# Second layer of a mixture of experts: rows gathered two units ahead, and one shared part for full and small units

## The chip, the cores and the metric

The kernel runs on one core of a Trainium2 chip. The metric is the device time of one execution in microseconds; the time of a kernel is the median of several runs. The engines are named as in the profile: PE is TensorE's matmul, PEld its weight load, DVE VectorE, ACT ScalarE, POOL GpSimd, SP SyncE.

## What is computed

The reference is attention with pooled queries, then two dense layers with a piecewise activation, then a second mixture of experts. Only the last step is touched by the change:

```python
N, D = x.shape                      # 2304 tokens, 512 columns
expert_idx = np.argmax(logits, axis=1)          # one of 8 experts for each token
gate_w = probs[np.arange(N), expert_idx]
for e in range(E):
    mask = expert_idx == e
    h = np.maximum(x[mask] @ w1[e], 0.0)        # w1[e]: 512 x 1024
    out[mask] = gate_w[mask, None] * (h @ w2[e])  # w2[e]: 1024 x 512
```

All is fp32. The kernel splits each fp32 operand into a high part, rounded to the format that PE multiplies fast, and a low part, the rest; a product is three matmuls (high by high, high by low, low by high).

## The kernel before, in words

The first stages write the rows of x to a table in HBM and scatter, for each token, a record (row number, output row, gate) into a second table that is sorted by expert. `units()` cuts this table into units of 256 rows of one expert; how many units there are (9 to 17) and which expert each has is known only at run time. The last unit of an expert can have 128 rows or fewer; it is then a small unit. A bit mask `half`, held in registers, says which units are small.

`Moe2.run` is written out for 17 units in a row; from unit 9 on each stands in a conditional on the number of units. What one unit does:

- `gather(u)` (L1202) has SP load 256 records (L1210), and POOL gather the 256 rows of x in two indirect DMAs of 128 rows (L1220) into a ring of four buffers `d_xg`, followed by a drain of POOL (L1206).
- `nxt(u)` (L1313) calls `gather(u)`, then reads the expert and a flag on SP and loads the four raw pieces of w1 (`load("1")`, L1182); the DMA is conditional, since the expert may be the one that is already there. `load("2")` does the same for w2.
- `split` (L1184) turns one of the eight pieces of a raw weight matrix into its high part (a cast on ACT, L1187) and its low part (a subtraction on DVE, L1188). There is one set of high and low parts: w1 of the next unit is split while the second product runs, w2 of the unit itself while its first product runs.
- `x_t` (L1235) transposes the next unit's rows on PE (L1227) and evicts them as a high part on ACT (L1231) and a low part on DVE (L1232).
- `hidden(f, x)` (L1241) makes an eighth of the hidden layer of a full unit in 12 matmuls of 256 columns (L1248), with a relu on ACT (L1250) and the low part on DVE (L1251).
- `half(x)` (L1253) makes the whole hidden layer of a small unit in 24 matmuls of 512 columns (L1262), with the rows on the partitions; `turn(i)` (L1270) transposes half of it (L1274).
- `outer(t, f)` (L1279) adds an eighth of the second product of tile t (128 rows) in three matmuls of 512 columns (L1284). `store` (L1288) scales the result on ACT (L1291) and has POOL scatter it to the output (L1292). A store waits for the landing of the one before.

The order is the program's order on each engine. In a unit u from 1 on, `nxt(u + 1)` comes first; then stands a conditional with two arms (L1335). The full arm has 8 `hidden`, 8 `outer(0, f)` with `x_t` behind f = 0 and a w1 split behind each f, a store, 8 `outer(1, f)`, a store. The small arm has `half`, 8 `outer(0, f)` with the second turn behind f = 1, `x_t` behind f = 5 and the same splits, and one store. Each engine evaluates the conditional by itself and jumps over the arm that is not taken. Unit 0 is always full and is written out apart; while it runs, the units are still being counted.

Of the kernel before, what the change touches and what calls it, by code (L numbers as in the profile page):

```python
# [11 lines left out]
U32 = mybir.dt.uint32  # L12
# [17 lines left out]
UMAX = UMIN + E  # L30
# [44 lines left out]
class Attention:  # L75
# [11 lines left out]
    def open(self, ctx):  # L87
        tc, nc = self.tc, self.nc

        def pool(name, bufs, **kw):  # L90
            return ctx.enter_context(tc.tile_pool(name=name, bufs=bufs, **kw))

        self.prep = tc.alloc_tile_pool(name="a_prep", bufs=1, side="right")
        self.vp = pool("a_v", 1)
        self.ktp = pool("a_kt", 2)
        self.sp = pool("a_s", 3)
        self.sm = pool("a_sm", 3)
        one = pool("a_one", 1)
        self.ps_s = pool("a_ps_s", 1, space=PSUM)
        self.ps_a = pool("a_ps_a", 1, space=PSUM)  # L100
        self.ps_b = pool("a_ps_b", 1, space=PSUM)
        self.ps_v = pool("a_ps_v", 2, space=PSUM)
        self.pth = one.tile([128, 9, RING], F32R, name="pth")
        self.ptl = one.tile([128, 9, RING], F32R, name="ptl")
        self.vh = one.tile([128, 18, 128], F32R, name="vh")
        self.avs = one.tile([128, 2 * NQ], F32, name="avs")

        self.qts = [one.tile([128, 2, QW], F32R, name=f"qt{i}") for i in range(2)]

        self.bd = [one.tile([128, 2, 128], F32R, name=f"bd{i}") for i in range(2)]  # L110
        self.kk = one.tile([128, 2, S], F32R, name="kk")
        self.r = one.tile([128, 32], F32, name="r")
        self.nc.vector.memset(self.r, 1.0)
# [1012 lines left out]
class Moe2:  # L1126
# [63 lines left out]
    def open(self, ctx):  # L1190
        def pool(name, **kw):
            return ctx.enter_context(self.tc.tile_pool(name=name, bufs=1, reuse_waits="tile", **kw))

        p, ps = pool("d_sb"), pool("d_ps", space=PSUM)
        self.ph = Ring(ps, 3, [128, 512], F32, "d_ph")
        self.pt = Ring(ps, 2, [128, 4, 128], F32, "d_pt")
        self.po = Ring(ps, 3, [128, 512], F32, "d_po")
        self.rec = Ring(p, 3, [128, 2, 4], U32, "d_rec")
        self.xg = Ring(p, 4, [128, DM], F32, "d_xg")
        self.ob = Ring(p, 4, [128, DM], F32, "d_ob")  # L1200

# [75 lines left out]
        nc.vector.tensor_sub(out=l, in0=p, in1=h.bitcast(F32))  # L1277

    def outer(self, t, f):  # L1279
        if f == 0:  # L1280
            self.o = self.po()
        s = slice(t * 128, t * 128 + 128)
        for q, (a, b) in enumerate(((0, "2h"), (0, "2l"), (1, "2h"))):
            self.nc.tensor.matmul(self.o, lhsT=(self.hh, self.hl)[a][f // 4][:, f % 4, s],  # L1284
                                  rhs=self.w[b, f // 2][:, f % 2],
                                  start=f == 0 and q == 0, stop=f == 7 and q == 2)
# [9 lines left out]
    def run(self, items):  # L1296

        nc, tc, rt = self.nc, self.tc, self.rt
        evs = []
        rec, x = self.rec0, self.xt0  # L1300

        def routing():
            while evs:
                evs.pop(0)()
            while items:
                f = items.popleft()
                if f is None:
                    return
                e = f()
                if e:  # L1310
                    evs.append(e)

        def nxt(u):  # L1313
            r = self.gather(u)
            e = nc.sync.value_load(rt.u[0:1, u, 1:2], min_val=0, max_val=E - 1)
            c = nc.sync.value_load(rt.u[0:1, u, 2:3], min_val=0, max_val=1)
            self.load("1", e, c)
            return r, e, c

        first = []  # L1320

        def step():
            if next(steps, None):
                first.extend(nxt(1))

        with ExitStack() as ifs:  # L1326
            for u in range(UMAX):
                if u >= UMIN:
                    ifs.enter_context(tc.If(total > u))
                more = u + 1 < UMAX  # L1330
                if more and u:
                    (rec1, xs1), e, c = nxt(u + 1)
                if u:
                    x1 = (self.xh(), self.xl()) if more else None
                    with tc.If((half & (1 << u)) == 0) as full:  # L1335
                        for f in range(8):
                            self.hidden(f, x)
                            self.split("2", f)
                        if more:
                            self.load("2", e, c)  # L1340
                        for f in range(8):
                            self.outer(0, f)
                            if more:
                                if f == 0:
                                    self.x_t(xs1, x1)
                                self.split("1", f)
                        self.store(rec, 0)
                        for f in range(8):
                            self.outer(1, f)
                        self.store(rec, 1)  # L1350
                    with full.Else():
                        self.half(x)
                        if more:
                            self.load("2", e, c)
                        for f in range(8):
                            self.outer(0, f)
                            if f == 1:
                                self.turn(1)
                            if more:
                                if f == 5:  # L1360
                                    self.x_t(xs1, x1)
                                self.split("1", f)
                        self.store(rec, 0)
                    x = x1
                else:
                    for f in range(2, 8):
                        self.hidden(f, x)
                        routing()
                        if f == 4:
                            steps = rt.units()  # L1370
                        for _ in range(min(3, f - 3)):
                            if not first:
                                step()
                        for i in {4: (2, 3), 5: (4, 5), 6: (6, 7)}.get(f, ()):
                            self.split("2", i)
                    for f in range(8):
                        self.outer(0, f)
                        step()
                    self.store(rec, 0)
                    self.load("2", *first[1:])  # L1380
                    for f in range(6):
                        self.outer(1, f)
                        step()
                    while not next(steps, 1):
                        pass
                    (rec1, xs1), e, c = first
                    for f in (0, 2, 4, 6):
                        self.split("1", f)
                    x = self.xh(), self.xl()
                    self.x_t(xs1, x, lambda: self.outer(1, 6))  # L1390
                    self.outer(1, 7)
                    total = nc.values_load(rt.u[0:1, 0, 2:3], min_val=UMIN, max_val=UMAX)
                    half = nc.values_load(rt.half[0:1, 0:1], min_val=0, max_val=(1 << (UMAX + 1)) - 1)
                    for f in (1, 3, 5, 7):
                        self.split("1", f)
                    self.store(rec, 1)
                if more:
                    rec = rec1

# [133 lines left out]
```

## Time and profile before

| | us |
|---|---|
| median of three runs | 1179.3 |
| lowest and highest run | 1173.73, 1179.88 |
| the profiled execution, its own time | 1178.18 |
| its span, first to last instruction | 1176.4 |

The profile is of one execution. Its times count from the start of the span. The granted clock of TensorE was 0.995 of full speed over the span. The second layer, from unit 1's start at about 938 us to the end, is a fifth of the span.

### The profile page before, as it was taken

The page shows a single profiled execution, that of the slowest core. Times are in us where ns is not written, and L with a number is a line of the kernel's source. Part 1 is how long each engine was busy: PE and PEld are TensorE (multiplying, and loading weights), DVE is VectorE, ACT ScalarE, POOL GpSimd, SP SyncE. Part 2 cuts the span into 40 slices and gives each one's busy share as a digit, 9 for nine tenths or more (in the row PEclk, how much of TensorE's full clock was granted, in tenths as well). Part 3 has the DMA queues.
Part 4 walks back from the last instruction along what each step waited for, and adds up shares of the span by engine and source line. Part 5 has one row for each costly group of instructions (what it writes and reads, how often), then busy time and mean ns, then how long its engine had stood idle before and what let it go on. Part 6 is the DMA issues. An engine that isn't in the chain of part 4 may idle for free. (4 is left out here: it accounts for less than half of the span.)

```text
span 1176.4 us, 21181 instructions
## 1 busy us (share of the span) xinstructions
PE 1135.4 (97%) x7315; PEld 1056.2 (90%) x7315; DVE 883.1 (75%) x1593; ACT 753.2 (64%) x1477; POOL 580.7 (49%) x499
## 2 busy tenths in 40 slices
PE   7999999999999999799999999999999999999997
PEld 6999999999999999799789999998889899887886
DVE  6898898899999998698866664764355776676765
ACT  5888888887878787555554445544435566566764
POOL 6998988887888885267762121112010221121212
PEclk9999999999999999899999999999999999999999
DMA  7777777786868758354532222120222121286443
GB/s 181 175 186 180 175 168 175 172 212 134 207 163 204 168 139 177 101 170 152 161 113 67 59 69 73 41 68 20 90 82 100 45 64 38 80 271 208 158 140 122
DMA packets 87877, 156.14 MB, mean 133 GB/s; under 512 B 26535, under 2 KB 44967, under 8 KB 87744
## 3 DMA queue, kind: packets, MB, share of 16 engines
q1 hardware_dynamic: 83040, 142.34, 45.4%
q0 software_dynamic: 4336, 11.58, 3.0%
q8 instruction: 67, 1.10, 0.4%
q10 hardware_dynamic: 368, 0.59, 0.2%
q14 instruction: 66, 0.54, 0.2%
HBM read 145.84 MB, written 20.08 MB: 141 GB/s over the span
## 5 line engine op out<-in xcount | busy, mean ns | idle before, releaser
L236 DVE TENSOR_SCALAR_CACHE_REDUCE e<-sc 128x1152 f32<-128x1152 f32 x144 | 194.7, 1352 | 24.3 <-PE sc L232 23.0
L243 ACT ACTIVATE e<-e,nm 128x1152 f32<-128x1152 f32 x144 | 183.6, 1275 | 9.0 <-DVE e L236 8.9
L232 PE MATMUL sc<-kT,qt 128*128 128x384 f32 x780 | 160.1, 340 | 11.7 <-DVE e L236 9.6
L270 ACT CAST pth<-pa 128x768 fp32r<-128x768 f32 (+2 forms) x160 | 116.3, 737 | 78.6 <-PE pa L261 78.4
L272 DVE TENSOR_TENSOR ptl<-pa,pth 128x768 fp32r<-128x768 f32 (+2 forms) x160 | 138.8, 876 | 17.7 <-ACT pth L270 5.5
L1188 DVE TENSOR_TENSOR e<-e,e 128x512 fp32r<-128x512 f32 x200 | 129.5, 688 | 28.3 <-ACT e L1187 12.3
L232 PEld LDWEIGHTS sc<-kT,qt 128*128 128x128 f32 x780 | 132.8, 189 | 14.5 <-DVE e L236 11.7
L596 DVE SCALAR_TENSOR_TENSOR u<-h,u 128x320 f32<-128x320 f32 (+1 forms) x112 | 55.7, 497 | 107.8 <-ACT u L595 107.4
L592 ACT ACTIVATE u<-h,half 128x320 f32<-128x320 f32 (+1 forms) x112 | 59.7, 533 | 109.5 <-PE h L577 109.3
L1284 PE MATMUL d_po<-e,e 128*128 128x512 f32 x504 | 121.0, 393 | 0.6 <-DVE e L1188 0.6
L261 PE MATMUL pa<-idf,e 128*128 128x128 f32 x864 | 117.6, 272 | 3.0 <-DVE ptl L272 3.0
L1187 ACT CAST e<-e 128x512 fp32r<-128x512 f32 x200 | 113.7, 619 | 0.6 <-issue 0.3
L609 PE MATMUL y<-wh,gh 128*128 128x512 f32 x288 | 113.9, 395 | 0.0
L609 PE MATMUL y<-wh,gl 128*128 128x512 f32 x288 | 113.7, 395 | 0.0
L609 PE MATMUL y<-wl,gh 128*128 128x512 f32 x288 | 113.6, 394 | 0.0
L261 PEld LDWEIGHTS pa<-idf,e 128*128 128x128 f32 x864 | 102.9, 140 | 8.3 <-issue 2.2
L1284 PEld LDWEIGHTS d_po<-e,e 128*128 128x128 f32 x504 | 92.6, 188 | 19.2 <-DVE e L1188 1.0
L1292 POOL DMA_INDIRECT out<-d_ob,d_rec x19 | 22.5, 1186 | 176.0 <-ACT d_ob L1291 119.3
L598 ACT CAST gh<-u 128x320 fp32r<-128x320 f32 (+1 forms) x112 | 52.3, 467 | 79.9 <-DVE u L596 79.9
L286 PE MATMUL av<-pth,vh 128*128 128x288 f32 x576 | 103.1, 306 | 0.0
L286 PE MATMUL av<-ptl,vh 128*128 128x288 f32 x576 | 102.2, 304 | 0.0
L577 PE MATMUL h<-xth,wh 128*128 128x320 f32 (+1 forms) x448 | 87.8, 318 | 8.3 <-DVE u L596 6.8
(258 smaller groups left out, 2533.8 us busy)
## 6 DMA issues: line engine op xcount, KB each, us to landing
e<-moe_w SPq DMA_DIRECT2D x104, 512.0 KB
kr<-k SPq DMA_DIRECT2D x63, 288.0 KB
qr<-q SPq DMA_DIRECT2D x62, 288.0 KB
kk<-kT SPq DMA_DIRECT2D x60, 288.0 KB
vr<-v SPq DMA_DIRECT2D x16, 576.0 KB
av_b<-avs SPq DMA_DIRECT2D x64, 128.0 KB
wi<-moe_w_in SPq DMA_DIRECT2D x16, 512.0 KB
wo<-moe_w_out SPq DMA_DIRECT2D x16, 512.0 KB
```

The costliest lines, as they stand in the source:

```text
L232: nc.tensor.matmul(s[:, j, 0:384], lhsT=a, rhs=b[:, 384 * j:384 * j + 384], start=i == 0, stop=i == len(mm) - 1)
L236: nc.vector.tensor_scalar(out=e.rearrange("p (a b) -> p a b", a=3), in0=s[:, :, 0:384], scalar1=-0.5 / D ** 0.5, scalar2=None, op0=ALU.mul ...
L243: self.nc.scalar.activation(e, e, AF.Exp, bias=d["nm"][:, t:t + 1], scale=-1.0, accum_out=d["sum"][:, t:t + 1])
L261: nc.tensor.transpose(p[:, c // 3, (c % 3) * 128:(c % 3) * 128 + 128], e[:, i * 128:(i + 1) * 128], idf)
L270: nc.scalar.copy(hi, p)
L272: nc.vector.tensor_sub(out=lo, in0=p, in1=hi.bitcast(F32))
L286: nc.tensor.matmul(box["t"][:, 0:GQ], lhsT=self.vh[:, h * 9 + i % 9], rhs=p[:, i % 9, c0:c0 + GQ], start=i == 0, stop=i == 17)
L577: nc.tensor.matmul(ps[:, :n], lhsT=a[:, k], rhs=b[:, k, h0:h0 + n], start=i == 0, stop=i == 11)
L609: self.nc.tensor.matmul(y, lhsT=a, rhs=b, start=j == 0 and q == 0, stop=j == NF - 1 and q == 2)
L1187: self.nc.scalar.copy(hi, r)
L1188: self.nc.vector.tensor_sub(out=lo, in0=r, in1=hi.bitcast(F32))
L1284: self.nc.tensor.matmul(self.o, lhsT=(self.hh, self.hl)[a][f // 4][:, f % 4, s], rhs=self.w[b, f // 2][:, f % 2], start=f == 0 and q == 0, ...
```

## The change

The rows of unit u + 2 are gathered in unit u, behind `nxt(u + 1)`, which no longer gathers; unit 0 ends with the gather of unit 2. The ring of records has four entries. The conditional's arms keep the first product, the load of w2 and the first two eighths of the second product of tile 0 (in the small arm with the second turn). The other six eighths, `x_t` (ahead of f = 4), the w1 splits (from f = 2 on) and the first store are written once, behind the arms. The second tile of a full unit stands in a second conditional. The PSUM bank of a second product is now taken by `run`, not by `outer`.

```diff
-        self.rec = Ring(p, 3, [128, 2, 4], U32, "d_rec")
+        self.rec = Ring(p, 4, [128, 2, 4], U32, "d_rec")
...
     def outer(self, t, f):
-        if f == 0:
-            self.o = self.po()
...
+        gathered = {}
+
         def nxt(u):
-            r = self.gather(u)
             e = nc.sync.value_load(rt.u[0:1, u, 1:2], min_val=0, max_val=E - 1)
             c = nc.sync.value_load(rt.u[0:1, u, 2:3], min_val=0, max_val=1)
             self.load("1", e, c)
-            return r, e, c
+            return e, c
...
             if next(steps, None):
+                gathered[1] = self.gather(1)
                 first.extend(nxt(1))
...
-                if more and u:
-                    (rec1, xs1), e, c = nxt(u + 1)
                 if u:
+                    if more:
+                        e, c = nxt(u + 1)
+                    if u + 2 < UMAX:
+                        gathered[u + 2] = self.gather(u + 2)
+                    rec1, xs1 = gathered.get(u + 1, (None, None))
                     x1 = (self.xh(), self.xl()) if more else None
+                    self.o = self.po()
                     with tc.If((half & (1 << u)) == 0) as full:
                         for f in range(8):
                             self.hidden(f, x)
                             self.split("2", f)
                         if more:
                             self.load("2", e, c)
-                        for f in range(8):
+                        for f in range(2):
                             self.outer(0, f)
-                            if more:
-                                if f == 0:
-                                    self.x_t(xs1, x1)
-                                self.split("1", f)
-                        self.store(rec, 0)
-                        for f in range(8):
-                            self.outer(1, f)
-                        self.store(rec, 1)
                     with full.Else():
                         self.half(x)
                         if more:
                             self.load("2", e, c)
+                        for f in range(2):
+                            self.outer(0, f)
+                        self.turn(1)
+                    for f in range(2, 8):
+                        if more:
+                            if f == 4:
+                                self.x_t(xs1, x1)
+                            for i in (0, 1) if f == 2 else (f - 1,):
+                                self.split("1", i)
+                        self.outer(0, f)
+                    if more:
+                        self.split("1", 7)
+                    self.store(rec, 0)
+                    with tc.If((half & (1 << u)) == 0):
+                        self.o = self.po()
                         for f in range(8):
-                            self.outer(0, f)
-                            if f == 1:
-                                self.turn(1)
-                            if more:
-                                if f == 5:
-                                    self.x_t(xs1, x1)
-                                self.split("1", f)
-                        self.store(rec, 0)
+                            self.outer(1, f)
+                        self.store(rec, 1)
                     x = x1
...
                     self.store(rec, 1)
+                    gathered[2] = self.gather(2)
```

## Rows read from the trace of the kernel before

**Rows 1.** The page's first part: busy us, share of span, instructions.

```profile
PE 1135.4 (97%) x7315; PEld 1056.2 (90%) x7315; DVE 883.1 (75%) x1593; ACT 753.2 (64%) x1477; POOL 580.7 (49%) x499
```

**Rows 2.** Stretches of units 3, 5, 7, 9, 11: us; busy PE, PEld, DVE, ACT, POOL; clock; DMA share.

```profile
984.13:1007.20 23.07, 23.07 (x153) 21.14 (x152) 15.04 (x26) 13.74 (x28) 4.34 (x4) 1.00 0.15 48
...
1030.45:1045.90 15.45, 12.94 (x66) 10.81 (x66) 10.44 (x17) 11.58 (x22) 3.39 (x3) 1.00 0.74 241
...
1069.10:1084.90 15.80, 13.24 (x66) 10.69 (x66) 10.72 (x18) 11.60 (x22) 3.22 (x3) 1.00 0.70 227
...
1107.80:1122.20 14.40, 13.30 (x66) 10.59 (x65) 10.76 (x18) 11.65 (x22) 3.06 (x3) 1.00 0.76 264
...
1145.10:1176.40 31.30, 23.68 (x153) 20.86 (x151) 15.13 (x26) 14.54 (x29) 5.90 (x5) 0.98 0.40 138
```

**Rows 3.** PE's waits from unit 1 on: us in total, times, longest.

```profile
PE d_ph L1262 <- ACT e L1187: 4.0, 2, 2.5
PE d_pt L1227 <- DMA d_xg<-y_rows,d_rec: 3.5, 4, 1.2
```

**Rows 4.** Timeline of PE: start, us, what, xcount, [idle before <- releaser].

```profile
1032.96 1.17 PE L1262 MATMUL d_ph<-e,d_xh 128*128 128x512 f32 x4 [2.51 <-ACT e L1187]
...
1039.00 1.54 PE L1284 MATMUL d_po<-e,e 128*128 128x512 f32 x6
...
1045.82 0.94 PE L1248 MATMUL d_ph<-d_xh,e 128*128 128x256 f32 x4
...
1070.61 1.17 PE L1262 MATMUL d_ph<-e,d_xh 128*128 128x512 f32 x4 [1.49 <-ACT e L1187]
...
1082.95 0.66 PE L1227 MATMUL d_pt<-idf,d_xg 128*128 128x128 f32 x4 [1.07 <-DMA d_xg<-y_rows,d_rec]
...
1107.81 1.08 PE L1262 MATMUL d_ph<-e,d_xh 128*128 128x512 f32 x4
...
1113.77 1.52 PE L1284 MATMUL d_po<-e,e 128*128 128x512 f32 x6
...
1119.45 1.44 PE L1227 MATMUL d_pt<-idf,d_xg 128*128 128x128 f32 x8 [0.97 <-DMA d_xg<-y_rows,d_rec]
...
1159.79 10.48 PE L1284 MATMUL d_po<-e,e 128*128 128x512 f32 x45
```

**Rows 5.** PE's branches at L1335, four windows: xcount, ns min/median/max, first and last start.

```profile
L1335 PEldq COMPARE_BRANCH  x2: 174/3200/6227, 1026.2 to 1026.6; - x2
...
L1335 PEldq COMPARE_BRANCH  x2: 312/2692/5072, 1064.9 to 1065.4; - x2
...
L1335 PEldq COMPARE_BRANCH  x2: 174/250/325, 1103.8 to 1104.2; - x2
...
L1335 PEldq COMPARE_BRANCH  x6: 66/128/312, 957.0 to 1003.6; - x6
```

**Rows 6.** The page's third part: packets, MB, share of 16 engines.

```profile
q8 instruction: 67, 1.10, 0.4%
```

**Rows 7.** Timeline of POOL in unit 7, and the landing of all gathers.

```profile
1073.82 1.00 POOL L1292 DMA_INDIRECT out<-d_ob,d_rec  x1 [7.73 <-DMA out<-d_ob,d_rec]
...
1076.67 0.97 POOL L1220 DMA_INDIRECT d_xg<-y_rows,d_rec  x1 [0.30 <-PE d_ph L1262]
...
DMA to landing us min/median/max: 3.2/3.9/6.5
```

**Rows 8.** Timelines of ACT and DVE in unit 9, behind the second turn.

```profile
1116.25 2.18 ACT L1187 CAST e<-e 128x512 fp32r<-128x512 f32 x4
...
1116.38 0.69 DVE L1277 TENSOR_TENSOR e<-d_pt,e 128x512 fp32r<-128x512 f32 x1
1116.99 2.49 DVE L1188 TENSOR_TENSOR e<-e,e 128x512 fp32r<-128x512 f32 x4
```

**Rows 9.** Timeline of POOL, the last two stores.

```profile
1165.88 1.20 POOL L1292 DMA_INDIRECT out<-d_ob,d_rec  x1 [11.01 <-ACT d_ob L1291]
1171.27 1.00 POOL L1292 DMA_INDIRECT out<-d_ob,d_rec  x1 [4.19 <-ACT d_ob L1291]
```

More of the change, by code (lines that the diff above doesn't have):

```diff
@@ L1375, in run @@
                             self.split("2", i)
+                    self.o = self.po()
                     for f in range(8):
@@ L1379, in run @@
                     self.store(rec, 0)
-                    self.load("2", *first[1:])
+                    self.load("2", *first)
+                    self.o = self.po()
                     for f in range(6):
@@ L1385, in run @@
                         pass
-                    (rec1, xs1), e, c = first
                     for f in (0, 2, 4, 6):
                         self.split("1", f)
+                    rec1, xs1 = gathered[1]
                     x = self.xh(), self.xl()
```

## The prediction

> **What bounds the kernel now.** The page comes first: PE is busy for 97% of the span [rows 1], so time can be won only where PE waits or where the program ends after it. The change touches the second layer alone. The table of its stretches, cut at the units' borders, shows which units run: unit 0, then 1 to 4 full, 5 small, 6 full, 7 small, 8 full, 9 small, 10 and 11 full. A full unit has no idle PE (23.07 us of 23.07); the small ones idle 2.5, 2.6 and 1.1 us, and the last stretch 7.6 us, most of it the program's end [rows 2]. The list of PE's waits from unit 1 on has two rows only: two waits before the first product of a small unit, 4.0 us, and four waits of the transposes for gathered rows, 3.5 us [rows 3]. The timeline places them: 2.51 us at the start of unit 5 and 1.49 at that of 7, but none at that of 9; 1.07 us before the second transposes of unit 7, 0.97 before the first of unit 9 [rows 4], and the remaining two, 1.5 us, in unit 11. These 7.5 us and the end are nearly all that the layer can give.
>
> The two waits at the start are put down to ACT's split, but that split is a w2 piece, which the first product does not read. The branches of the test show more. In the stretch of unit 5's start, one PE branch takes 6.23 us, in that of unit 7 one takes 5.07, in that of unit 9 the longest is 0.33 [rows 5]. PE's sequencer runs some 4 us ahead of its matmuls (the branch began at 1026.6, PE went idle at 1030.45), so about 2.5 and 1.5 us show. In the before kernel these are the jumps past the full arm: 152 matmuls, each a load and a multiply, 304 instructions.
>
> **The change part by part.**
>
> *Jumps.* After it, a small unit jumps past 96 + 6 matmuls, 204 instructions, and later past the second tile's 24, 48 instructions; a full unit jumps past the small arm's 38 matmuls, 76 instructions (it was 64, 128). The page counts 67 instruction packets of 1.10 MB in the main instruction queue [rows 6], 16 KB each. Spread over PE's 14,630 loads and multiplies and the some 1,900 that were jumped over, 1.10 MB is about 66 bytes each, so a packet is about 250 instructions. A jump of 304 can pass a whole packet, one of 204 or less cannot: its target is in the packet being run or the next. The next one is fetched early if its packet was entered early, and before a small unit stand 24 matmuls of the second tile, 5.6 us of PE (45 take 10.48) [rows 4]. So the price of the 204 jump lies between 0 (as at unit 9) and what it is now (4.0 us for all); I take 0, because the two slow jumps are the longest kind, and the kind of 128, taken at the end of each full unit, stayed at or under 0.33 us [rows 5]. **Gain 4.0 us.** The new tests add at most 0.33 us of sequencer time each and lie behind the 4 us that PE's sequencer is ahead; if that cover were gone, 11 units times 0.33 would be 3.6 us.
>
> [...]
>
> *Gathers two units ahead.* Unit u+1's rows were asked for at the start of unit u, behind the last store of unit u-1: in unit 7 that store was issued at 1073.82, the second gather at 1076.67, and its rows ended PE's wait at 1082.95 [rows 4, 7]. Now they are asked for a unit earlier, 14 us or more, where landing takes 3.2 to 6.5 us [rows 7]. The queues that the step passes: on SP the record load now stands behind the next unit's four w1 loads and in front of its w2 loads, on POOL nothing changes place except that unit 1 issues two gathers in a row, one drain more before its store. If the record lands late, POOL's store behind it is late, not PE, which has a unit to spare. The buffers of x were read in the unit before, and records have a fourth. The four waits go: **gain 3.5 us.** Unit 0's two waits, before unit 1's rows, stay as they are.
>
> *Transposes and w1 splits in the shared part.* In a full unit, the transposes move from the first to the fifth product and the splits begin at the third. ACT has 8 casts and 2 evictions, about 5.4 us, DVE 8 subtractions of 0.62 and 2 evictions, 6.3 us; both end some 8.4 us after the hidden products, and the next unit's first matmul comes 11.9 us after. **Nothing**, hidden by the second tile; without that cover it is the small unit's case.
>
> There it can cost. PE's own work: 5.96 us of first products with a turn (1107.81 to 1113.77) and 6.82 from there to the next unit (1039.00 to 1045.82) [rows 4]: 12.78 us. In both kernels splits can start only when the small arm's products have read w1; in the new one the transposes' evictions come before five splits, not three, and the first split comes behind the turn (a wait after the two arms must hold for the longer one, so I let it wait for the small arm's end). Counted from the unit's start, with 0.54 us per cast and the casts beginning at 8.4 as at 1116.25 [rows 8], ACT: turn evicted 8.5, three casts 10.1, two evictions 11.1, five casts 13.7. DVE, at 0.62 per split and some 0.65 per eviction: turn 9.3, three splits 11.1, evictions 12.3, five splits 15.4 [rows 8]. The next unit's twelfth matmul needs w1's seventh piece, DVE 14.75; PE unhindered is there at 14.1 (12.78 and eleven matmuls of 0.12: a full unit's 23.07 us less 48 second products at 0.233 and a us of transposes leaves 11 for its 96) [rows 2, 4]. So PE waits about 0.8 us behind a small unit, 13.6 us in all. Before, their stretches were 15.45, 15.80 and 14.40 us [rows 2], 45.65; after, 40.7 to 40.8. Bounds: no wait 38.3, twice my wait 43.1. **Small units: gain 4.9 us, 2.5 to 7.3.** This contains the jumps (4.0) and two of the gathers' waits (2.0), less 1.1 that the new order gives back.
>
> *Other edits.* The banks of the second product are taken in the same turn of three, two a unit and not three; the record ring costs nothing but space.
>
> *The end.* In unit 11 the first store goes out when ACT's splits are done, now 3.8 us before PE's end, before 4.4 (1165.88 against 1170.27) [rows 4, 9]; the second store waits for its landing (POOL sat 4.19 us) and went out 1.0 us after PE's end. It will be about 1.3: **loss 0.3 us**, at most 0.9 if nothing of it hides.
>
> **Sum.** Against the profiled execution, 1178.18 us (span 1176.4 and 1.8 around it): small units -4.9, unit 11's gathers -1.5, end +0.3, together -6.1: 1172.1. The median shown is 1.1 us over the profiled one, so 1173.2 by it; I say 1172.5.
>
> **Rivals.**
> 1. The jumps stay slow: the 204 jump still meets a packet that isn't there. For it: weights fill the DMA queues just there, and the two waits are at the starts of units 5 and 7, where DMA was busy 74 and 70% of the unit. Against it: unit 9 had 76% and did not wait [rows 2]. The gain is then 6.1 - 4.0 = 2.1 us: 1176.1. [...]
> 2. The small unit becomes DVE's: if the transposes come late for the third split and their evictions slip behind the fourth, the seventh piece is 0.6 us later and its wait with it; with another 0.2 for ACT's part, PE waits 1.6 us, not 0.8, in each of the three: -6.1 + 2.4 = -3.7: 1174.5. For it: DVE's end at 15.4 already lies 2.6 us behind PE's own; against: nothing else waits for DVE there before the next unit's first relu.
> 3. Slower: the new jump in the middle of each full unit, past 76 instructions, misses its code. Full units 1 to 4, 6, 8, 10 and 11 are eight. A missed jump showed 2.5 us of PE in unit 5; the forecast is used up at three, and at five (12.5 us) the kernel is slower by 0.5%: 1184.6. Against it: jumps of 128 at the same rate never missed. [...]
> 4. The gathers are not early, because the record load sits behind 2 MB of w1: then 3.5 us return, -2.6: 1175.6. Against it: the landing has a whole unit.
>
> **Chances.** Forecast 0.55, rivals 1 and 4 together 0.24, rival 2 0.13, rival 3 0.08. About 0.5% (5.9 us) is what a measurement of this kernel tells from no change; the runs shown lie 1173.7 to 1179.9. The forecast's own range, 1169.5 to 1175, straddles that bound, with some three quarters of it beyond, as the bounds allow more gain than loss. Faster 0.44, same 0.49, slower 0.07. The range takes in the best case (no waits in the small units, -8.5: 1169.7, and 2.5 us of the runs' scatter) and rivals 1, 2 and 4 with theirs: 1167 to 1178.5.
>
> **What would show it.** Right: no wait of the transposes for gathered rows from unit 1 on; PE's branches at the small units' starts under 0.5 us, and no idle PE there; small units of some 13.6 us, DVE's subtraction as the releaser just behind; full units still 23.1; the last store about 1.3 us after PE's end. Wrong: branches of some us anywhere on PE, above all in the middle of full units; or waits of the first shared product for ACT or DVE, which would mean that leaving the arms costs a synchronization that I took to be nothing.

## The result

The changed kernel took 1169.1 us in the median of five runs (1167.89 to 1170.56), against 1179.1 us of the kernel before beside it (1173.73 to 1179.88). The ratio is 0.9913, with an interval from 0.9893 to 0.9934: faster, by 0.9%. A second series, on another chip, gave 1169.7 us against 1178.6, ratio 0.9922 [0.9897, 0.9948]. The forecast was 1172.5, its range 1167 to 1178.5.

The profiled execution of the changed kernel took 1167.89 us, its span is 1166.2. First the page's busy times, then the same stretches as [rows 2]: units 3, 5, 7, 9, and 11 with the end.

```profile
PE 1132.8 (97%) x7315; PEld 1055.1 (90%) x7315; DVE 884.1 (76%) x1593; ACT 752.2 (65%) x1477; POOL 581.7 (50%) x501
```

```profile
982.20:1005.30 23.10, 23.10 (x154) 21.16 (x153) 15.03 (x26) 13.66 (x28) 4.23 (x4) 1.00 0.16 47
1028.30:1041.65 13.35, 12.93 (x65) 10.45 (x64) 10.44 (x17) 11.98 (x23) 3.03 (x3) 1.00 0.75 245
1064.60:1077.96 13.36, 12.94 (x65) 10.43 (x64) 10.47 (x17) 12.00 (x23) 3.46 (x3) 1.00 0.80 268
1100.90:1114.40 13.50, 12.95 (x66) 10.42 (x64) 10.61 (x18) 12.12 (x23) 3.54 (x3) 1.00 0.74 258
1137.20:1166.20 29.00, 23.23 (x153) 20.95 (x151) 15.04 (x26) 14.35 (x29) 5.22 (x5) 0.94 0.43 137
```

The instructions are the same (POOL's two more are the gathers of one more unit), and their busy time is nearly so. The small units fell from 15.45, 15.80 and 14.40 us [rows 2] to 13.35, 13.36 and 13.50, and PE is idle for 0.42 to 0.55 us in each of them. The list of PE's waits from unit 1 on (us in total, times, longest) has one row, where [rows 3] has two:

```profile
PE d_ph L1248 <- ACT e L1187: 1.4, 3, 0.6
```

No transpose waits for gathered rows any more, and no small unit starts late. What is left stands behind the small units, as PE's timeline of unit 5 shows:

```profile
1028.30 1.08 PE L1262 MATMUL d_ph<-e,d_xh 128*128 128x512 f32 x4
...
1034.25 1.55 PE L1282 MATMUL d_po<-e,e 128*128 128x512 f32 x6
...
1037.46 1.04 PE L1227 MATMUL d_pt<-idf,d_xg 128*128 128x128 f32 x8
1038.25 2.98 PE L1282 MATMUL d_po<-e,e 128*128 128x512 f32 x12
1041.65 0.73 PE L1248 MATMUL d_ph<-d_xh,e 128*128 128x256 f32 x4 [0.42 <-ACT e L1187]
```

PE's sequencer at the two tests (L1339 the first, L1364 the second; from unit 1 to the middle of unit 11; xcount, ns min/median/max, first and last start):

```profile
L1339 PEldq COMPARE_BRANCH  x18: 66/174/431, 945.9 to 1147.1; - x18
```

```profile
L1364 PEldq COMPARE_BRANCH  x17: 63/169/219, 950.3 to 1133.1; - x17
L1364 PEldq ALU_OP  x8: 36/36/36, 950.2 to 1092.1; - x8
L1364 PEldq EVENT_SEMAPHORE  x3: 51/51/51, 1041.3 to 1113.9; - x3
```

The branches of 6.23 and 5.07 us [rows 5] are gone; no branch at these two tests takes more than 0.43. The three semaphore instructions at L1364 stand at the end of the second conditional, and only where its arm is jumped over, in the three small units. The first stands at 1041.3, where the last product of unit 5 has just ended (1038.25 + 2.98 = 1041.23).

Each unit is cut where its first product starts; where PE waits ahead of a small unit, the unit begins with that wait. Set against the forecast:

| stretch, us | before | after | change | forecast |
|---|---|---|---|---|
| units 5, 7, 9 (small) | 45.41 | 40.25 | -5.2 | -4.9 |
| unit 11 | 25.18 | 23.24 | -1.9 | -1.5 |
| behind PE's last product | 6.09 | 5.75 | -0.3 | +0.3 |
| units 1 to 4, 6, 8, 10 | 161.73 | 160.94 | -0.8 | 0 |
| the layer | 238.41 | 230.17 | -8.2 | -6.1 |

The two profiled executions differ by 10.3 us. The other 2 us lie ahead of unit 1, which starts at 937.95 in the one and at 936.01 in the other. In a second profile of the changed kernel it starts at 939.9, and the layer takes 230.5 us: the layer repeats, and what is ahead of it scatters by some 4 us (unit 1 starts between 935.2 and 939.9 in the profiles of the kernels below, with either layout). So the change is worth about 8 us by these profiles, 10.0 and 8.9 us by the medians of the two series; the interval of the second is some 6 to 12 us. That the rest of the 10 is not its is likely, but not shown.

### The profile page after: what moved, and what is told of

It is laid out like the page before. It is cut to its first block, busy times and chain, and to the rows that moved or that the text cites. A ratio compares the mean times of both kernels' runs of the same rounds, so it can differ in the third digit from the quotient of the medians.

```text
span 1166.2 us, 21384 instructions
## 1 busy us (share of the span) xinstructions
PE 1132.8 (97%) x7315; PEld 1055.1 (90%) x7315; DVE 884.1 (76%) x1593; ACT 752.2 (65%) x1477; POOL 581.7 (50%) x501
## 4 chain that ended last, share of the span: by engine, by line
PE 74%; DVE 6%; issue 6%; POOL 5%; DMA 5%; ACT 2%; SPq 1%; POOLq 0%; DVEq 0%; ACTq 0%
PE h L577 13%; PE y L609 13%; PE sc L232 12%; PE av L286 10%; PE pa L261 7%; PE d_po L1282 7%; PE d_ph L1248 6%; PE pb L261 3%; DVE wf L462 2%; PE d_ph L1262 1%; DMA wi<-moe_w_in 1%; POOL wl L451 1%; DVE wf L466 1%; DMA out<-d_ob,d_rec 1%; DVE ptl L272 1%
```

## The experiments

Twelve kernels ran. Each time is a median, and each ratio is to runs of the kernel before on the same chip. "The layer" is from unit 1's first product to the end of the span, in the one profiled execution: 238.4 us before, 230.2 after.

**The changed kernel again (c_after).** 

> The changed kernel once more, as a control beside the others. From unit 1's start to the end it took 230.2 us in its first profile against 238.4 before; the rest of the 10 us lay ahead of unit 1, in code that the change does not touch (unit 1 started 1.9 us earlier). If that part is scatter between executions, unit 1's start moves by about 2 us again from profile to profile, with either kernel. If it belongs to the change, unit 1 starts near 936.0 us again here, and in the kernels below that keep the change's layout, while the before layout starts near 938.

Measured: 1169.7 us (1168.48 to 1172.13), ratio 0.9922 [0.9897, 0.9948], the layer 230.5; the three waits behind small units are there again with 1.4 us.

**The gathers alone (e2_gather_only).** The kernel before with its arms whole, and the rows gathered two units ahead:

```diff
 # before.py, nxt(u) and run
-            r = self.gather(u)
...
-                    (rec1, xs1), e, c = nxt(u + 1)
+                    e, c = nxt(u + 1)
+                if u and u + 2 < UMAX:
+                    gathered[u + 2] = self.gather(u + 2)
...
+                    gathered[2] = self.gather(2)
```

> The kernel before with the gathers two units ahead and nothing else: the arms stay whole. Theory: the waits of the transposes for rows go (3.5 us), the waits at the starts of units 5 and 7 (4.0 us) and PE's branches of 5 to 6 us there stay; 3 to 4 us under the kernel before. Rival (the waits at units 5 and 7 came from late rows or stores and not from the jump): those waits go too, 7 us under before.

Measured: 1175.1 us (1170.9 to 1177.29), ratio 0.9962 [0.9941, 0.9984], 3.5 us less than the kernel before. PE's waits, its branches in two windows (starts of units 5 and 7), and PE's timeline and a window at unit 7's start:

```profile
PE d_ph L1262 <- ACT e L1187: 5.3, 2, 3.1
```

```profile
L1340 PEldq COMPARE_BRANCH  x2: 174/2987/5800, 1025.0 to 1025.3; - x2
...
L1340 PEldq COMPARE_BRANCH  x2: 315/3514/6712, 1063.3 to 1063.7; - x2
```

```profile
1070.61 1.94 PE L1262 MATMUL d_ph<-e,d_xh 128*128 128x512 f32 x4 [3.13 <-ACT e L1187]
```

```profile
1069.00:1074.50 5.50, 3.90 (x10) 3.14 (x11) 2.30 (x4) 1.26 (x3) 1.99 (x2) 0.69 0.54 156
```

The waits for rows are gone and the two slow jumps remain, as the theory has it, so the two groups of waits have separate causes. In this one execution the jumps even cost more, 5.3 us of idle PE, and behind the 3.13 us of idle time four products took 1.94 us, not 1.17 as in [rows 4]: the granted clock had fallen, to 0.69 in the stretch shown. So the layer of this execution is 237.8 us, only 0.7 less than before; the 3.5 us are a difference of medians, with an interval of some 2 to 7.

**One unit ahead in the new layout (e1_one_ahead, e9_one_ahead_first).** The changed kernel with the rows gathered one unit ahead, in e1 behind the next unit's w1 loads on SP, in e9 ahead of them as before the change:

```diff
 # after.py; e1 puts the gather behind nxt, e9 in front of it
+                        gathered[u + 1] = self.gather(u + 1)
                         e, c = nxt(u + 1)
-                    if u + 2 < UMAX:
-                        gathered[u + 2] = self.gather(u + 2)
...
-                    gathered[2] = self.gather(2)
```

> The changed kernel with its shared part, but rows gathered one unit ahead again, at the start of the unit. Theory (the gathers' waits and the jumps' waits are separate gains): the transposes' waits for rows return, 1 us or more in each of units 5, 7 and 9, where the transposes now stand 1.4 us earlier in a small unit, and less in full units, where they stand 2.8 us later; 3 to 6 us longer than the changed kernel, still no idle PE at the small units' starts and branches under 0.5 us. Rival (the gathers were hidden and all the gain is the shared part): within 1 us of the changed kernel.

> The changed kernel with the rows gathered one unit ahead and the record load ahead of the next unit's w1 loads, as it stood before the change. Theory (e1_one_ahead was slow because its record load queued behind 2 MB of w1): POOL's waits for records shrink to under 2 us each, PE's waits for rows are some 2 to 4 us, as in the kernel before, and the time is 1172 to 1175. Rival (one unit of lead is too little for the shared layout wherever the record load stands): PE's waits for rows stay near the 10 us of e1_one_ahead and the time is 1183 to 1188.

Measured: e1 1187.3 us (1185.97 to 1189.06), ratio 1.0073 [1.0047, 1.01]; e9 1190.1 us (1188.4 to 1191.57), ratio 1.0093 [1.0061, 1.0125]. Both are slower than the kernel before, and some 18 to 21 us slower than the changed one, where e1's theory had 3 to 6. In e1 POOL did wait for records:

```profile
POOL d_xg L1220 <- DMA d_rec<-table: 9.2, 3, 6.3
POOL out L1290 <- DMA d_rec<-table: 7.5, 1, 7.5
```

In e9 POOL never waits for them, and it is no faster. So my theory, that e1 was slow because its record load queued behind w1, fell; the rival's waits of about 10 us came, and the time lies above its range of 1183 to 1188. e9's waits of PE, PE's timeline in unit 5 and windows of it (us, five engines, granted clock, DMA share) show what it was:

```profile
PE d_pt L1227 <- DMA d_xg<-y_rows,d_rec: 10.4, 6, 3.2
PE d_ph L1248 <- PEq L1363: 1.4, 3, 0.6
PE d_pt L1227 <- DVE d_xl L1232: 1.4, 1, 1.4
```

```profile
1041.99 0.70 PE L1227 MATMUL d_pt<-idf,d_xg 128*128 128x128 f32 x4 [2.65 <-DMA d_xg<-y_rows,d_rec]
1044.05 1.09 PE L1227 MATMUL d_pt<-idf,d_xg 128*128 128x128 f32 x4 [1.36 <-DVE d_xl L1232]
1044.79 5.09 PE L1282 MATMUL d_po<-e,e 128*128 128x512 f32 x12
```

```profile
1030.00:1039.30 9.30, 9.30 (x45) 7.36 (x43) 6.39 (x11) 7.92 (x15) 3.44 (x3) 1.00 0.74 251
...
1044.80:1049.20 4.40, 4.40 (x12) 3.45 (x11) 3.41 (x6) 3.18 (x6) 0.00 (x0) 0.50 0.20 52
```

The shared part has the transposes 9.2 us behind a small unit's start (1028.30 to 1037.46 in the changed kernel's rows above); in the small arm of before they were due some 1.5 us later (1119.45 less the wait of 0.97, against 1107.81 [rows 4]). Rows that were about 1 us late there are 2.65 us late here, a second wait of 1.36 us follows, and then the granted clock is 0.50: twelve products take 5.09 us, not 2.98. Unit 5 takes 20.28 us, not 13.35. The new layout by itself would have been a loss. It needs the second unit of lead.

**The length of the jump (e3, e4, e7, e8, e11).** All are the changed kernel with one more conditional at the start of units 2, 3, 4, 6, 8 and 10, whose matmuls are never run:

```diff
+                    if u in (2, 3, 4, 6, 8, 10):
+                        with tc.If((half & (1 << 17)) > 0):   # e3, e4: total > 40
+                            p = self.ph()
+                            for i in range(152):    # e3, e7: 152; e4, e8: 102; e11: 219
+                                nc.tensor.matmul(p, lhsT=..., rhs=..., start=True, stop=True)
```

> The changed kernel with a third conditional, never taken, ahead of the test in units 2, 3, 4, 6, 8 and 10: PE has to jump past 152 matmuls, 304 instructions, as it did past the full arm in the kernel before. No work is added. Theory (the long jump past a whole packet of instructions is what cost 4 us): some of these six branches of PE take 3 to 6 us, those whose target lies beyond the next packet, and PE idles up to 2.5 us behind them where the weights' traffic is heavy; 2 to 8 us over the changed kernel. [...]

> The same with 102 matmuls in the arm that is never taken, 204 instructions, the length of the changed kernel's own jump in a small unit. Theory: a target is never beyond the next packet, so the branches stay under 0.5 us unless the packet was entered just before; within 1 us of the changed kernel. Rival (any taken jump over some length, or a further conditional in itself, costs): about the same addition as the run with 304.

Measured: e3 1171.9 us (1170.09 to 1172.88), ratio 0.9928 [0.9903, 0.9953], e4 1171.2 us (1170.4 to 1174.18), ratio 0.9928 [0.9905, 0.9952]; the layer 232.6 and 232.5. They did not answer the question. The trace has no branch at L1339: that the total stays under 40 was known when the kernel was built, and the arm is not in the program. What is left is the semaphore instruction at the conditional's end, and it has a price by itself. In e3's list of waits:

```profile
PE d_ph L1248 <- PEq L1339: 2.5, 5, 0.6
```

Each full unit ahead of such an instruction takes 0.4 to 0.7 us longer, and the layer 2.4 us. The next two ask with a bit of the mask, which only the run knows.

> Units 2, 3, 4, 6, 8 and 10 begin with an arm of 152 matmuls (304 PE instructions) that is never taken, by a test that only the run can answer (bit 17 of the mask); its matmuls would only fill a bank that nobody reads. Theory (a jump of 304 passes a packet of instructions, and PE waits for the next one): most of the six branches take 4 to 7 us, 1.5 to 2.5 us of each show as idle PE, the layer is 240 to 247 us and the time 1178 to 1186. Rival (the length is nothing; the two slow jumps of the kernel before came from their place): branches stay under 0.5 us, only the synchronisation at the end of each test remains, 2 to 3 us in all as in e3_dead_304, and the time is 1171 to 1173.

> The same with 102 matmuls, 204 PE instructions. Theory (a jump of 204 or less ends in the packet that is being run or the next): branches under 0.5 us, the layer within 1 us of the 232.5 of e4_dead_204, the time 1171 to 1173. Rival (any jump past a few dozen matmuls at a unit's start is slow): as e7_jump_304, 1178 to 1186, and the jumps in the changed kernel are fast for another reason than their length.

Measured: e7 1178.7 us (1175.47 to 1180.98), ratio 0.9993 [0.997, 1.0017], the layer 237.9; e8 1175.4 us (1172.55 to 1178.43), ratio 0.9974 [0.995, 0.9998], the layer 236.6. PE's branches of e7, then of e8:

```profile
L1339 PEldq COMPARE_BRANCH  x6: 332/353/834, 956.8 to 1118.6; - x6
```

```profile
L1339 PEldq COMPARE_BRANCH  x6: 223/332/434, 956.9 to 1120.3; - x6
```

By its time e7 lies in the theory's range, but by its layer (240 to 247 us) and its branches the theory as I had put it fell: a jump of 304 alone took 0.83 us at most. e8 missed its theory too, which had the layer within 1 us of 232.5. Part of the longer layers is six synchronisations, of 0.4 to 0.5 us behind full units and 1.0 to 1.2 behind small ones. And once in each kernel PE ran dry among a unit's first products with nothing else to wait for, 2.14 us in e7 and 1.70 in e8; here is e8's:

```profile
1047.59 0.98 PE L1248 MATMUL d_ph<-d_xh,e 128*128 128x256 f32 x7 [1.70 <-issue]
```

In e8 a packet of the main instruction queue had ended at 1046.10, in e7 one at 1120.79, where PE went on at 1122.17: 1.4 to 1.5 us before in both, as in the slow branches below. So one of six jumps had a price at either length, not in its branch but in the products behind it. What the slow jumps of before have besides their length is a neighbour. [rows 5] has two branches in each window, under half a microsecond apart: the short one is the jump past the small arm at the end of the full unit, the long one the jump past the full arm. Together they pass 128 + 304 = 432 instructions.

> As e7_jump_304 with 219 matmuls, 438 PE instructions. In the kernel before, the slow jump past the full arm (304) follows within half a microsecond on the jump past the small arm (128), 432 in all; in e7_jump_304 the 304 stood alone and its branches took 0.33 to 0.83 us. Theory (what counts is the whole distance that is passed at once, against packets of some 250 instructions): at least four of the six branches take 2.5 to 7 us, 1 to 3 us of each show as idle PE, the layer is 245 to 256 us and the time 1184 to 1196. Rival (distance is nothing; the pair of jumps is slow for another reason): branches under 1 us as in e7_jump_304 and 1175 to 1181.

Measured: 1190.5 us (1189.42 to 1192.39), ratio 1.0107 [1.0077, 1.0136], the layer 252.1. Its branches, its waits, and PE's timeline and a window behind the fourth of them:

```profile
L1339 PEldq COMPARE_BRANCH  x6: 352/3603/5772, 956.3 to 1130.2; - x6
```

```profile
PE d_ph L1248 <- PEq L1339: 16.8, 6, 6.6
```

```profile
1049.60 1.22 PE L1248 MATMUL d_ph<-d_xh,e 128*128 128x256 f32 x4 [6.57 <-PEq L1339]
```

```profile
1049.00:1052.00 3.00, 2.40 (x11) 2.41 (x12) 0.00 (x0) 0.00 (x0) 0.00 (x0) 0.50 0.45 153
```

Five of the six branches took 3.55 to 5.77 us, one 0.35. The theory had 1 to 3 us of idle PE behind each. Instead the two slow ones behind full units (3.57 and 3.64 us) hid behind the sequencer's lead, with 0.42 us of idle PE as at a mere synchronisation, and the three behind small units (5.77, 3.83 and 3.55 us) showed in full: 6.57, 4.56 and 4.42 us. There the second conditional, jumped over, had just emptied the queue, and the lead was gone.

The distance decides: 304 alone gave no slow branch in six, 438 gave five. That the place of the start decides as well is worked out, not tested, since no run moved a jump of one length. By the prediction's estimate of 250 instructions a packet (in the kernel before, from 25 to 915 us, one ends every 254 loads and multiplies in the median, 182 to 324), a jump of 304 passes a whole packet from about one start in five (54 of 250), one of 432 or 438 from about three in four: in the kernel before and in e2_gather_only it was two of three, here five of six, and in e7 none of six, where about one was due. An instruction packet does move inside such a branch: in the kernel before, the DMA view of the stretch 1065.3 to 1070.5, unit 7's branch, has one.

```profile
q8 instruction: 1, 0.02, 1.4%
```

The packets' own times in the traces show that the branch waits for it. In the fourteen profiles, 23 branches of PE took over 3 us: nine at the first test, in the kernel before, e2_gather_only and e11, and in each profile the jump past the units that don't run, at the layer's end. In all 23 a packet of this queue ends inside the branch, and the branch ends 1.36 to 1.55 us after it. In none of the other 540 branches does a packet end. A packet also moves just behind most short jumps (within 3.6 us in all six of e8); there the branch does not wait for it. And the next packet comes early: in the kernel before, a second one ended 3.62 us after the first at unit 5's slow branch and 3.16 at unit 7's, and PE began 17 and 15 loads and multiplies between the two.

**The wait behind small units (e5, e6, e10).** The prediction had put a wait there down to DVE's splits of w1. e5 puts the splits in another order, e6 moves the transposes three products later:

```diff
 # e5
-                            for i in (0, 1) if f == 2 else (f - 1,):
+                            for i in (0, 2) if f == 2 else ((4, 6, 1, 3, 5)[f - 3],):
 # e6
-                            if f == 4:
+                            if f == 7:
                                 self.x_t(xs1, x1)
```

> The changed kernel with the w1 splits of the shared part in the order 0, 2, 4, (transposes) 6, 1, 3, 5, 7: the even pieces are those that the next unit's first matmuls read. Theory (the new order of splits holds PE behind a small unit): PE's waits at the starts of units 6, 8 and 10, 1.4 us in the list of waits, go, and the kernel is 1 to 2 us under the changed one. Rival: raw pieces are freed in pairs, so the next w1 loads start up to 1.5 us later and arrive late; then the same time or more, with splits waiting for weights.

> The changed kernel with the transposes of the next rows ahead of the eighth product of tile 0, not the fifth; the splits' order is unchanged, two of them stand behind the transposes and not five. Theory (in a small unit DVE's and ACT's chain of three to five splits behind the evictions decides when the next unit can go on): the chain's length stays, but the evictions now end about 2 us later and only two splits follow, so the seventh piece comes at much the same time; PE's wait behind a small unit stays within 0.5 us of what it was, in full units nothing changes; within 1.5 us of the changed kernel. Rival (the place of the evictions alone decides): each small unit is 1 us or more shorter or longer.

Measured: e5 1168.4 us (1167.96 to 1170.81), ratio 0.9921 [0.9895, 0.9947]; e6 1170.9 us (1169.17 to 1171.31), ratio 0.9914 [0.9887, 0.9941]. Neither can be told from the changed kernel, and the small units stay at 13.36 to 13.51 and 13.38 to 13.52 us. In e5 the three waits are unchanged, 1.4 us. In e6 two of them are put down to the sequencer:

```profile
PE d_ph L1248 <- PEq L1364: 0.8, 2, 0.4
PE d_ph L1248 <- ACT e L1187: 0.6, 1, 0.6
```

So e5's theory fell, and the order of the splits is not what holds PE. e10 takes the second conditional away: the second tile goes into the full arm, ahead of the first.

```diff
 # full arm; the small arm gets the same three splits behind turn(1), the rest x_t at f == 3
+                    o0, o1 = self.po(), self.po()
...
+                        self.o = o1
+                        for f in range(8):
+                            self.outer(1, f)
+                            if more and f in (1, 3, 5):
+                                self.split("1", f // 2)
+                        self.store(rec, 1)
+                        self.o = o0
                         for f in range(2):
                             self.outer(0, f)
...
-                    with tc.If((half & (1 << u)) == 0):
-                        self.o = self.po()
-                        for f in range(8):
-                            self.outer(1, f)
-                        self.store(rec, 1)
```

> The changed kernel without the second conditional: the second tile's product and its store stand in the full arm, ahead of the first tile's first two eighths, with three of the w1 splits; the small arm has the same three splits behind its turn. Theory (the 1.4 us that PE waits behind small units is the synchronisation of leaving the second conditional): that wait is gone, small units take 12.9 to 13.1 us and not 13.4, full units stay, the time is 1 to 1.5 us under the changed kernel's. Rival (the jump past the full arm, now 252 PE instructions, meets missing code): branches of some us at the starts of units 5, 7 and 9, 2 to 4 us of idle PE, slower than the changed kernel. Second rival (the wait belongs to the w1 splits): about 0.5 us stays at the start of each unit behind a small one.

Measured: 1170.5 us (1170.01 to 1171.99), ratio 0.9925 [0.9902, 0.9949], the layer 231.9; small units 13.30, 13.34 and 13.29 us. Its branches, its waits from unit 1 on, and PE's timeline at the end of unit 5 and the start of 6:

```profile
L1339 PEldq COMPARE_BRANCH  x19: 66/174/1260, 937.3 to 1153.5; - x19
```

```profile
PE d_pt L1227 <- issue: 0.6, 2, 0.3
PE d_pt L1227 <- DVE e L1277: 0.3, 1, 0.3
```

```profile
1039.14 0.66 PE L1227 MATMUL d_pt<-idf,d_xg 128*128 128x128 f32 x4 [0.31 <-issue]
1039.56 3.66 PE L1282 MATMUL d_po<-e,e 128*128 128x512 f32 x15
1043.06 0.64 PE L1248 MATMUL d_ph<-d_xh,e 128*128 128x256 f32 x4
1043.53 0.63 PE L1248 MATMUL d_ph<-d_xl,e 128*128 128x256 f32 x4
1044.00 1.41 PE L1248 MATMUL d_ph<-d_xh,e 128*128 128x256 f32 x8
```

The wait between the units is gone with the conditional, as the synchronisation theory says, but not the time: it had small units of 12.9 to 13.1 us and 1 to 1.5 us in all. For 0.31 us comes back at the transposes, which now follow the second turn closely, and products nine to sixteen of unit 6 take 1.41 us, where eight take 1.07 to 1.11 elsewhere: there they do wait, some 0.3 us, as the prediction had them wait for DVE (its last four splits start at 1042.61 and take 2.48, so the seventh piece, the third of them, is there at about 1044.5; the twelfth product was due at about 1044.4). Unit 5 is shorter by 0.05 us, units 6 and 10 are longer than in the changed kernel by 0.5 and 0.6, and the end by 0.8. A jump past 252 instructions took up to 1.26 us and shows nowhere on PE. No version tried here beats the changed kernel by more than the runs' scatter.

## Why the prediction was right, point by point

- **What bounds the kernel, and the place of the gain: right.** The time went from the two groups of waits in [rows 3], and nearly all of it from the small units and unit 11.
- **Jumps, 4.0 us: right in size, half right in mechanism, and in part by luck.** The slow branches are gone. The distance passed counts (e11 against e7), and the slow branches waited for an instruction packet (23 of 23, above). But it was hardly the 304 by itself: that passes a packet of 250 from one start in five, and in e7 none of six was slow, while before two of three were. With the jump past the small arm just ahead it is 432, and for that two of three fits. That the two add up is inferred from the equal distance of e11; no run put two shorter jumps in a row. The change shortens the jump to 204, and the 42 products of the shared part and the second tile now stand between it and the jump past the small arm; which of the two was needed is not separated, since e7's 304, set apart, had no slow branch either. The price of 0 that I took for the 204, out of 0 to 4.0, held at the three places where the changed kernel has it. That is luck in part: in e8 one of six jumps of 204 left PE dry for 1.70 us. The jump in the middle of a full unit (rival 3) never took over 0.43 us.
- **Gathers, 3.5 us: right.** The waits are gone in e2_gather_only and in the changed kernel, and e2_gather_only gave 3.5 us by medians, though with a wide interval. In POOL's timeline of the changed kernel rows are asked for a unit early; here is unit 7 with unit 9's rows, then the first gather of unit 10's:

```profile
1071.32 0.98 POOL L1220 DMA_INDIRECT d_xg<-y_rows,d_rec  x1 [0.30 <-issue]
...
1083.71 1.24 POOL L1220 DMA_INDIRECT d_xg<-y_rows,d_rec  x1 [2.48 <-DMA d_rec<-table]
```

  Rival 4's mechanism, a record load late behind w1, is there as well (2.48 us of POOL), and the unit of lead hides it, as the prediction said. What the prediction did not see is that in the new layout one unit of lead would have cost 18 to 21 us, not 3.5: it priced the two parts apart, and they hang together.
- **The order of splits, -1.1 us: right in size by luck, wrong in cause.** I gave back 0.8 us a small unit for DVE's seventh piece of w1. The units came out at 13.35 to 13.52, where I had 13.6. DVE's times were as worked out (its last five splits began at 1040.50, row below, 12.2 us behind unit 5's start, where I had 12.3), but PE comes to the seventh piece only about when it is ready, since it has already lost 0.42 to 0.56 us to the synchronisation at the end of the skipped second conditional. That is a step that I put at nothing: I had named a synchronization as a sign of being wrong, but for the arms of the first test, and I had put the new tests behind the 4 us that PE's sequencer is ahead. At the end of the second conditional that lead is gone. The list of waits puts the wait down to ACT's cast, but e5, where the casts of the even pieces come earlier, has it unchanged; e3 has waits like it where nothing but the synchronisation was added, e6 has two of the three at the sequencer, e10 has them gone, and has a wait of some 0.3 us at the splits in their place. Two different costs of much the same size stand in each other's shadow, and so the size came out. DVE's timeline in unit 5 of the changed kernel:

```profile
1037.50 1.88 DVE L1188 TENSOR_TENSOR e<-e,e 128x512 fp32r<-128x512 f32 x3
1039.30 1.28 DVE L1232 TENSOR_TENSOR d_xl<-d_pt,d_xh 128x512 fp32r<-128x512 f32 x2
1040.50 3.09 DVE L1188 TENSOR_TENSOR e<-e,e 128x512 fp32r<-128x512 f32 x5
```

- **The end, +0.3 us: wrong by 0.6.** The last store went out 1.05 us behind PE's last product (1161.48 against 1160.43), where I had 1.3, and its landing and what follows were shorter.

```profile
1156.40 1.26 POOL L1290 DMA_INDIRECT out<-d_ob,d_rec  x1 [12.11 <-ACT d_ob L1289]
1161.48 1.00 POOL L1290 DMA_INDIRECT out<-d_ob,d_rec  x1 [3.82 <-ACT d_ob L1289]
```

- **The sum, -6.1 against -8.2 for the layer.** No term is off by more than 0.8 us; the 2.1 us are small ones of one sign: the end 0.6, the small units 0.3, unit 11 0.4 and the other full units 0.8. The measured median lies 10 us below, and the remaining 2 us stand ahead of the layer, where two profiles of one kernel differ by as much. The forecast lay close to the bound of 0.5%, and the small terms, with the part ahead of the layer, decided on which side of it the kernel came out.

## What to carry to other kernels

Add up the instructions that a run-time jump passes together with a jump just ahead of it, and set the sum against the size of an instruction packet (some 250 instructions by the estimate here; five of six branches were slow at 438, none at 304); code that both arms share makes the jumps shorter and sets them apart. Before moving a consumer forward, look how late its data already are: a layout that is 9 to 10 us faster than the old one with two units of lead is 9 to 12 us slower with one. And a skipped conditional is not free: here its end waited until PE's queue was empty, 0.42 to 0.56 us of idle PE, and a slow jump just behind it had nothing left to hide behind (a branch of 5.77 us, 6.57 us of idle PE).

## What the runs showed of the hardware

- **PE's granted clock was down behind the longer waits, and such a wait cost more than itself.** After 2.51 us idle the products ran at the granted clock of 1.00 (four in 1.17 us, [rows 4]); after 3.13 us four took 1.94 us and the stretch had 0.69 (e2_gather_only); after 6.57 us the clock was 0.50, and so it was after waits of 2.65 and 1.36 us in short order (e11_jump_438, e9_one_ahead_first). By the lists of waits e11 has 15.4 us more idle PE than the changed kernel, and its layer is 21.9 us longer; e9 has 11.8 more, and 19.7.
- **At the end of a conditional whose arm was skipped, PE's queue was empty**: in the changed kernel the semaphore instructions there start at 1041.3, 1077.6 and 1113.9, the last products ahead of them end at 1041.23, 1077.54 and 1113.84. That is 0.42 to 0.56 us of idle PE each time, and 0.4 to 0.7 us a unit in e3, where nothing was skipped at all.
- **The slow jumps waited for an instruction packet**: all 23 branches over 3 us end 1.36 to 1.55 us after a packet of the queue has ended. At one distance, 438, branches took 0.35 or 3.55 to 5.77 us.
- **Two jumps had their price later**: 1.70 and 2.14 us of idle PE among the products behind a jump of 204 and one of 304, whose branches were short.
